# Moving the decay of two chunks from the values to the keys in a fused retention and feed-forward kernel

**Chip, cores, metric.** One core of one Trainium2 chip. The metric is the device time of one execution in microseconds (us), median of several runs; lower is better.

## The reference

Eight heads with a fixed decay each, over four sequences of 768 tokens with 64 values per head; the result goes through a multiplicative feed-forward layer.

```python
gamma = 1.0 - 2.0 ** (-5.0 - np.arange(H))
for t in range(S):
    state = gamma * state + outer(k[:, :, t], v[:, :, t])
    y[:, :, t] = scale * q[:, :, t] @ state
x = y as (tokens, heads * 64)                 # 3072 x 512
out = (((x @ w1) * (x @ w2)) @ w3) @ w_out
```

## The kernel before

The sequence is cut into chunks of 128 tokens. A chunk needs its keys in fp16 (`k16`), the keys transposed and padded (`KP`), scores masked to fp16 (`am`), and padded values (`VP`). The decay inside the chunk is a factor per token and head, `VS` or `VS2`. It is multiplied into the values, once, and so it is in both the output (`am` times `VP`) and the state (`k16` times `VP`). It could just as well be multiplied into the keys: scores and state both contain the keys exactly once. W3 and W_out are folded into one matrix at the start of the kernel.

The change concerns chunks 2 and 3, in the hand-ordered part between the start of the kernel and its steady loop. Each engine runs its instructions in the order of these lines, so this order is the schedule of every engine. A "row group" is one `by_rows` call: the product with a quarter of the rows of W1 or W2. `pa` are copies of W1's sums out of PSUM, where TensorE's results stand ("accumulator copies"). ScalarE, VectorE and GpSimd are `nc.scalar`, `nc.vector` and `nc.gpsimd`; `cast_to(dst, src, True)` is a copy on VectorE, `False` one on ScalarE.

```python
def pair_casts(n, moved, names="kv", eng=None):   # half of a chunk's 128 tokens
    eng = eng or (nc.vector if moved else nc.gpsimd)
    if "k" in names:  ... copy or cast 64x512 of the keys to k16s[n] ...
    for r in range(2 if "v" in names else 0):     # even heads, odd heads
        eng.tensor_tensor(VP[n % 3][to, :, r, ...], values, VS2 broadcast, MULT)
...
by_rows(W1, ps, 0 and 1)                          # feed-forward of chunks 0, 1
for n in (2, 3):
    pair_casts(n, False, "k")                     # GpSimd
    pair_casts(n, True, "k", nc.scalar)
by_rows(W1, ps, 2)                                # "third row group"
transposes(2)
by_rows(W1, ps, 3)
transposes_front(3, "psK")
nc.gpsimd.tensor_copy(W2[0][:, :], w2_st[0][:, :])
pair_casts(2, False, "v")
pair_casts(3, False, "v")
...                                               # pa[0..2] out of PSUM
scores(2, between=lambda: pair_casts(2, True, "v"))
cast_to(pa[3], ps[3], True)
transposes_back(3)
cast_w(W2, w2_st, 1, False)                       # ScalarE; then 2 and 3
...
by_rows(W2, ps, 0); outputs(2, "psK"); scores(3); by_rows(W2, ps, 1); t_new = kv(2, "psY")
pair_casts(3, True, "v")
...                                               # f1.a_unit between W2's row groups
outputs(3, "psA1"); f1.a_unit(6, "psA0"); casts(4); Tst[0] = kv(3, "psK")
f0.o_unit(0)                                      # "first output unit"
```

## Time and profile before

| | before |
|---|---|
| time, median of 3 runs | 194.74 us (194.6 to 195.18) |
| span of the profiled execution | 193.1 us |
| busy: TensorE, VectorE, ScalarE, GpSimd | 184.1, 117.0, 103.3, 83.6 us |
| third row group of W1 ends (the next work starts) | 35.20 us |
| first output unit starts | 46.66 us |
| from there to the end | 146.43 us, TensorE never waiting |

How to read it: TensorE (PE) is busy nearly throughout, so the kernel is as long as TensorE's work plus its holes. A change in chunks 2 and 3 acts between 35.20 and 46.66 us. I call these 11.46 us "the stage".

### The profile page before, as it was taken

The numbers are of one execution on the slowest core, as the hardware profiler recorded it, in microseconds if no ns is written. First come the engines' busy times: TensorE is split into PE (matmuls) and PEld (weight loads), VectorE is DVE, ScalarE is ACT, GpSimd is POOL, SyncE is SP. The second block draws the span as 40 slices with busy tenths as digits, with TensorE's granted clock in tenths as the row PEclk, the third lists the DMA queues.
The fourth block names the chain that finished last, engine by engine and source line by source line (L and its number), as shares of the span: only waits on it lengthen the run. The fifth ranks groups of instructions, "written<-read, shape, count | busy, mean of one in ns | idle before, by whom it ended". The sixth has DMA issues, their size and how long they took to land.

```text
span 193.1 us, 4713 instructions
## 1 busy us (share of the span) xinstructions
PE 184.1 (95%) x1785; PEld 139.8 (72%) x1785; DVE 117.0 (61%) x220; ACT 103.3 (54%) x198; POOL 83.6 (43%) x144
## 2 busy tenths in 40 slices
PE   6698999979999999999999999999999999999993
PEld 2234557778797789777977797788777877887752
DVE  3225479699587758656665676565656665753220
ACT  6478598972454465354635463555355545533322
POOL 7600257728864737476252742863426432200000
PEclk9999999999999999999999999999999999999999
DMA  6999999998999999999999989969979930111104
GB/s 207 349 389 398 326 377 355 368 266 198 235 204 221 199 231 237 144 247 211 231 273 187 223 188 223 206 149 270 199 178 201 206 94 19 59 54 54 38 28 154
DMA packets 84007, 40.54 MB, mean 210 GB/s; under 512 B 61329, under 2 KB 78993, under 8 KB 83985
## 3 DMA queue, kind: packets, MB, share of 16 engines
q1 hardware_dynamic: 83984, 40.25, 88.5%
q8 instruction: 14, 0.23, 0.5%
q14 instruction: 9, 0.07, 0.2%
HBM read 29.36 MB, written 6.29 MB: 185 GB/s over the span
## 4 chain that ended last, share of the span: by engine, by line
PE 81%; DMA 10%; ACT 4%; DVE 2%; SPq 1%; issue 0%
PE psF L537 39%; PE psO L563 21%; DMA q<-in_q_dram 6%; PE psA L466 5%; DMA stg<-in_moe_w_out_dram 5%; PE psY L506 3%; PE psY L507 3%; PE psF L760 2%; PE psY L509 2%; PE psK L489 2%; SPq L62 1%; PE psG L537 1%; PE psO L580 1%; ACT w3o L241 1%; PE psG L760 1%; DVE vp L329 1%
## 5 line engine op out<-in xcount | busy, mean ns | idle before, releaser
L537 PE MATMUL psF<-xt,w 128*128 128x256 f16 (+1 forms) x736 | 85.0, 266 | 0.0
L537 PEld LDWEIGHTS <-w 128*128 128x128 f16 x768 | 68.2, 98 | 7.2
L553 DVE TENSOR_TENSOR ht<-pa,psF 128x256 f16<-128x256 f32 x88 | 36.6, 416 | 22.4 <-PE psF L537 13.1
L547 ACT COPY pa<-psF 128x256 f32<-128x256 f32 x84 | 31.3, 372 | 33.4 <-PE psF L537 33.0
L471 DVE TENSOR_TENSOR am<-psA,keep 128x512 f16<-128x512 f32 x48 | 30.9, 684 | 21.4 <-PE psA L466 21.3
L563 PE MATMUL psO<-w3o,ht 128*128 128x512 f16 x184 | 43.3, 379 | 0.0
L498 POOL TENSOR_TENSOR t<-s,GS 128x512 f16<-128x512 f32 x15 | 19.3, 1285 | 38.7 <-DVE s L497 38.7
L568 ACT ACTIVATE osb<-psO 128x512 f32<-128x512 f32 x23 | 13.7, 598 | 37.3 <-PE psO L563 37.3
L563 PEld LDWEIGHTS <-ht 128*128 128x128 f16 x184 | 17.8, 98 | 16.9 <-DVE ht L806 0.2
L383 POOL TENSOR_TENSOR vp<-v,VS 128x256 f16<-128x256 f32 x40 | 23.8, 617 | 6.9 <-DMA v<-in_v_dram 3.3
L514 DVE TENSOR_TENSOR xt<-psY,YS 128x512 f16<-128x512 f32 x24 | 17.8, 742 | 4.1 <-PE psY L509 3.8
L506 PE MATMUL psY<-am,vp 128*128 128x128 f16 x96 | 16.8, 219 | 0.9 <-POOL vp L329 0.7
L507 PE MATMUL psY<-am,vp 128*128 128x128 f16 x96 | 16.7, 219 | 0.6 <-DVE vp L329 0.6
L466 PEld LDWEIGHTS <-kp 128*128 128x128 f16 x192 | 12.5, 98 | 4.5 <-DVE kp L239 0.2
L338 POOL CAST q<-q 128x1024 f16<-128x1024 f32 x10 | 10.6, 1057 | 11.9 <-DMA q<-in_q_dram 11.9
L379 POOL CAST k<-k 128x512 f16<-128x512 f32 x20 | 12.3, 613 | 5.5 <-DMA v<-in_v_dram 2.4
L497 DVE TENSOR_TENSOR s<-psK,t 128x512 f32<-128x512 f32 x16 | 11.0, 688 | 2.8 <-PE psK L489 2.5
L262 DVE COPY w3t<-psW 128x1024 f16<-128x1024 f16 x8 | 5.5, 690 | 10.9 <-PE psW L270 8.5
L466 PE MATMUL psA<-qTd,kp 128*128 128x128 f16 x144 | 11.1, 219 | 0.0
L509 PE MATMUL psY<-qTd,t 128*128 128x128 f16 x60 | 10.8, 219 | 0.0
L440 ACT COPY kp<-kT 64x512 f16<-64x512 f16 x17 | 10.5, 618 | 0.4
L441 ACT COPY kp<-kT 64x512 f16<-64x512 f16 x17 | 10.5, 615 | 0.4
(87 smaller groups left out, 193.9 us busy)
## 6 DMA issues: line engine op xcount, KB each, us to landing
stg<-in_moe_w_dram SPq DMA_DIRECT2D x16, 512.0 KB, 8.5
q<-in_q_dram SPq DMA_DIRECT2D x12, 512.0 KB, 5.4
out_dram<-osb SPq DMA_DIRECT2D x23, 256.0 KB, 3.2
k<-in_k_dram SPq DMA_DIRECT2D x20, 256.0 KB, 5.3
v<-in_v_dram SPq DMA_DIRECT2D x20, 256.0 KB, 5.5
stg<-in_moe_w_out_dram SPq DMA_DIRECT2D x4, 512.0 KB, 8.2
stg<-in_k_dram SPq DMA_DIRECT2D x2, 512.0 KB, 9.9
stg<-in_v_dram SPq DMA_DIRECT2D x2, 512.0 KB, 9.7
```

The costliest lines, as they stand in the source:

```text
L383: nc.gpsimd.tensor_tensor(vp[:, :, r, r * 64 : r * 64 + 64], v32[:, :].rearrange("j (p s e) -> j p s e", s=2, e=64)[:, :, r, :], VS[:, :]. ...
L466: nc.tensor.matmul(ps[:, i, r, :], lhsT=kp[:, p, r, :], rhs=queries(n, p), start=True, stop=True)
L471: nc.vector.tensor_tensor(am[:, half * 2 : half * 2 + 2, :, :].rearrange("j p s i -> j (p s) i"), ps[:, :, :, :].rearrange("j p s i -> j ( ...
L498: eng.tensor_tensor(t16[:, :, :], s32[:, :, :], GS[:, :, :], MULT)
L506: nc.tensor.matmul(ps[:, p, :], lhsT=vp[:, p, 0, :], rhs=am[:, p, 0, :], start=True, stop=False)
L507: nc.tensor.matmul(ps[:, p, :], lhsT=vp[:, p, 1, :], rhs=am[:, p, 1, :], start=False, stop=(c == 0))
L509: nc.tensor.matmul(ps[:, p, :], lhsT=Tst[0][:, p, :], rhs=queries(n, p), start=False, stop=True)
L514: nc.vector.tensor_tensor(XT[n // 2][:, :, n % 2 * C : (n % 2 + 1) * C].rearrange("p a (i t) -> p a t i", t=2), ps[:, :, :].rearrange(orde ...
L537: nc.tensor.matmul(ps[:, i * w : (i + 1) * w], lhsT=W[d][:, (f + i) * 128 : (f + i + 1) * 128], rhs=XT[self.tok0 // TB][:, d, c0 : c0 + w] ...
L547: nc.scalar.copy(self.pa[f][:, :], ps[:, :])
L553: nc.vector.tensor_tensor(self.HT[:, f : f + TB // self.width, :].rearrange("p f n -> p (f n)"), self.pa.pop(f)[:, :], ps[:, :], MULT,)
L563: nc.tensor.matmul(psO[:, :], lhsT=self.HT[:, f, tb * 128 : (tb + 1) * 128], rhs=W3O[f][:, :], start=(f == 0), stop=(f == 7),)
```

## The change

The intent: at chunk 2's output TensorE waits for values that GpSimd and VectorE are still scaling. So the decay goes onto the keys; values become plain copies, which ScalarE can do too. All four key products are on VectorE, as are both copies of chunk 2's padded keys. ScalarE is relieved of two key casts and of one cast of W2.

```diff
+    def scaled_keys(n, moved):
+        ...
+        nc.vector.tensor_tensor(k16s[n][half], keys, VS2 broadcast, MULT)     # 64x512
+    def plain_values(n, moved, copy):
+        ...
+        copy(VP[n % 3][half, even and odd heads in one pattern], values)      # 64x512
     def transposes_back(n):
-        nc.scalar.copy(kp[0:64, :, 0, :], ps[0:64, :, :])
+        cast_to(kp[0:64, :, 0, :], ps[0:64, :, :], n == 2)
         cast_to(kp[64:128, :, 1, :], ps[64:128, :, :], n == 2)
...
-    for n in (2, 3):
-        pair_casts(n, False, "k")
-        pair_casts(n, True, "k", nc.scalar)
+    scaled_keys(2, False)
+    scaled_keys(2, True)
+    scaled_keys(3, False)
     by_rows(W1, ps, 2)
+    by_rows(W1, ps, 3, blocks=(0, 3))
     transposes(2)
-    by_rows(W1, ps, 3)
-    transposes_front(3, "psK")
+    scaled_keys(3, True)
+    by_rows(W1, ps, 3, blocks=(3, 8))
     nc.gpsimd.tensor_copy(W2[0][:, :], w2_st[0][:, :])
-    pair_casts(2, False, "v")
-    pair_casts(3, False, "v")
+    plain_values(2, False, nc.gpsimd.tensor_copy)
+    plain_values(3, False, nc.gpsimd.tensor_copy)
     cast_to(pa[0], ps[0], False)
-    cast_to(pa[1], ps[1], True)
+    cast_to(pa[1], ps[1], False)
     cast_to(pa[2], ps[2], False)
-    scores(2, between=lambda: pair_casts(2, True, "v"))
+    scores(2)
     cast_to(pa[3], ps[3], True)
-    transposes_back(3)
-    cast_w(W2, w2_st, 1, False)
+    plain_values(2, True, nc.scalar.copy)
+    transposes(3, "psK")
+    nc.gpsimd.tensor_copy(W2[1][:, :], w2_st[1][:, :])
...
-    pair_casts(3, True, "v")
+    plain_values(3, True, nc.gpsimd.tensor_copy)
...                                  # PSUM banks renamed in outputs, scores, a_unit, kv
```

More of the change, by code (lines that the diff above doesn't have):

```diff
@@ L342, in q_cast @@
         q16s[m] = q16
+    def scaled_keys(n, moved):
+        m, c = divmod(n, 2)
+        rows = slice(c * 64, c * 64 + 64)
+        t = 1 - c if moved else c
+        if n not in k16s:
+            k16s[n] = att.tile([128, 512], HP, tag="k16", name="k16", bufs=3)
+        nc.vector.tensor_tensor(
+            k16s[n][t * 64 : t * 64 + 64, :].rearrange("i (h d) -> i h d", d=D),
+            pair_in["k", m][rows, :].rearrange("i (h t d) -> i h t d", t=2, d=D)[:, :, t, :],
+            VS2[rows, t, :].unsqueeze(2).broadcast_to((64, H, D)), MULT,
+        )
+    def plain_values(n, moved, copy):
+        m, c = divmod(n, 2)
+        rows = slice(c * 64, c * 64 + 64)
+        t = 1 - c if moved else c
+        dst = VP[n % 3][t * 64 : t * 64 + 64, :, :, :]
+        dst = bass.AP(dst.tensor, dst.offset, [list(dst.ap[0]), [256, NP], [192, 2], [1, 64]])
+        copy(
+            dst,
+            pair_in["v", m][rows, :].rearrange("j (p s t e) -> j p s t e", s=2, t=2, e=64)[:, :, :, t, :],
+        )
     def q4_cast(half, on_act):
@@ L792 @@
     by_rows(W2, ps, 0)
-    outputs(2, "psK")
-    scores(3)
+    outputs(2, "psA0")
+    scores(3, ("psA1", "psK"))
     by_rows(W2, ps, 1)
@@ L797 @@
     Tst[0] = t_new
-    pair_casts(3, True, "v")
+    plain_values(3, True, nc.gpsimd.tensor_copy)
     f1 = ffn[1]
-    f1.a_unit(0, "psK")
+    f1.a_unit(0, "psA0")
     by_rows(W2, ps, 2)
-    f1.a_unit(2, "psA0")
+    f1.a_unit(2, "psK")
     by_rows(W2, ps, 3)
-    f1.a_unit(4, "psK")
+    f1.a_unit(4, "psA0")
     for i in range(4):
@@ L807 @@
     outputs(3, "psA1")
-    f1.a_unit(6, "psA0")
+    f1.a_unit(6, "psK")
     casts(4)
-    Tst[0] = kv(3, "psK")
+    Tst[0] = kv(3, "psA0")
     f0.o_unit(0)
```

## The prediction

> **What bounds the kernel now.** I read the page first, then the waits of TensorE, then the timelines of single engines around the two chunks that change. The page's row of busy tenths puts TensorE at 9 in nearly every slice after the first fifth, and its chain ends so:
>
> ```profile
> PE 184.1 (95%) x1785; PEld 139.8 (72%) x1785; DVE 117.0 (61%) x220; ACT 103.3 (54%) x198; POOL 83.6 (43%) x144
> PE 81%; DMA 10%; ACT 4%; DVE 2%; SPq 1%; issue 0%
> ```
>
> TensorE is the bound, so a change to the other engines can win only what TensorE now loses to waits. After 46.5 us the view of waits lists none for TensorE. Between 22 and 50 us it lists four, all inside the code that leads to chunk 2's output or just before it:
>
> ```profile
> PE psY L506 <- POOL vp L329: 0.7, 1, 0.7
> PE psY L507 <- DVE vp L329: 0.6, 1, 0.6
> PE psT L450 <- ACT k L324: 0.4, 1, 0.4
> PE psY L506 <- DVE am L471: 0.2, 1, 0.2
> ```
>
> The third belongs to chunk 0, which the change leaves alone. The other three are the target. In TensorE's timeline (start, length, engine, line, operands):
>
> ```profile
> 37.83 0.38 PE L760 MATMUL psG<-xt,w 128*128 128x256 f16 x2
> 38.89 0.22 PE L506 MATMUL psY<-am,vp 128*128 128x128 f16 x1 [0.68 <-POOL vp L329]
> 39.70 0.22 PE L507 MATMUL psY<-am,vp 128*128 128x128 f16 x1 [0.59 <-DVE vp L329]
> ...
> 40.33 0.22 PE L506 MATMUL psY<-am,vp 128*128 128x128 f16 x1 [0.19 <-DVE am L471]
> ...
> 40.66 0.61 PE L466 MATMUL psA<-qT,kp 128*128 128x128 f16 x8
> ```
>
> Chunk 2's output could have begun at 38.05 (37.83 and two matmuls 0.11 apart) and the next work began at 40.66: 2.61 us for twelve matmuls that take 0.70 in chunk 3 (starts 45.29 to 45.99). So 1.91 us are lost there, and 0.21 in chunk 2's scores (start 36.52 to the next work at 37.18, 0.66 against 0.45 for chunk 3's, waiting for the padded keys). The ceiling of the gain is 2.12 us, 1.1% of 194.74: "faster by over 2%" is out of reach even if every wait goes.
>
> Why are the values late? They land at about 37.3, and then two engines scale them at once:
>
> ```profile
> 37.33 2.70 POOL L329 TENSOR_TENSOR vp<-stg,VS 64x256 f16<-64x256 f32 x4 [0.52 <-DMA stg<-in_v_dram]
> 38.07 0.72 DVE L329 TENSOR_TENSOR vp<-stg,VS 64x256 f16<-64x256 f32 x1
> 38.72 0.83 DVE L329 TENSOR_TENSOR vp<-stg,VS 64x256 f16<-64x256 f32 x1
> 43.40 0.42 DVE L329 TENSOR_TENSOR vp<-stg,VS 64x256 f16<-64x256 f32 x1
> 43.51 1.44 POOL L498 TENSOR_TENSOR t<-s,GS 128x512 f16<-128x512 f32 x1 [3.48 <-DVE s L497]
> 43.74 1.49 DVE L329 TENSOR_TENSOR vp<-stg,VS 64x256 f16<-64x256 f32 x1
> ```
>
> The same VectorE instruction takes 0.42 us when it starts first and up to 1.49 beside a GpSimd one; the last of them ends at 45.23, 0.28 after GpSimd's at 44.95.
>
> **What the skill says.** The Trainium skill, "SBUF — State Buffer", section "SBUF: two separate sides": VectorE and GpSimd share one SBUF port pair as an exclusive lock; a VectorE instruction with two SBUF inputs and a GpSimd instruction that reads SBUF block each other for the whole instruction, and the first to start has it. The trace agrees: the blocked end minus the holder's end is 0.28, which is 0.42 less some 0.14 of start-up. It also holds the other way: the first key cast on GpSimd took 0.80 instead of 0.61, because VectorE's product t<-s,GS (33.87 for 0.69) was running. The trace before has no plain GpSimd copy that blocks a VectorE product, so that half rests on the skill. "VectorE: DVE Perf Modes", section "Two Vector instructions with no wait between them", says that an instruction starts only after all earlier ones if an operand begins in another group of 32 partitions than before. In the trace, VectorE's instructions on equal partitions overlap by 0.09 us, and the first one after a change of half starts 0.03 after the end before it (38.07 after 38.04). The new instructions change halves nearly every time, so I add 0.03 and no overlap.
>
> **The change part by part.**
> Removed for chunks 2 and 3: eight half-value products (four on GpSimd at 0.61 uncontended, four on VectorE at 0.42), two key casts on ScalarE (0.62 each) and two on GpSimd (0.61). One 0.58 key copy out of PSUM leaves ScalarE, as does one 1.05 weight cast; ScalarE takes over one 0.58 accumulator copy (0.69 on VectorE).
> Added on GpSimd: three plain 64x512 copies; from its cast of the same form I take 0.61 each, and the 1.04 weight cast. Added on ScalarE: one copy, 0.62. None of these sets the end: values are then ready at about 38.4, well before the masked scores.
> Added on VectorE: four 64x512 products with two SBUF inputs, 0.69 each (from the 128x512 product at 33.87; the free size counts), and a padded-key copy of 0.43. These are the new path: TensorE's transposes, scores and masking all wait for them in series. Before, two engines cast keys in parallel from 34.2 to 35.7.
>
> VectorE in the new order, with no lock met: it is free at about 34.47 (keys landed at 34.2). Product 2a 34.47 to 35.16; 2b 35.19 to 35.88; 3a 35.91 to 36.60; two padded-key copies to 37.52; 3b 37.55 to 38.24. The transposes of chunk 3 then start at 38.28. Nothing on TensorE can pass them. What follows up to the first output unit, from the starts in the timeline: transposes 0.22, four W2 row groups 3.48, two outputs 1.40, chunk 3's scores 0.45, two key-value products 0.44, four a units 1.80; sum 7.79. It begins at 46.07, against 46.66 before: a gain of 0.59, so 194.15.
>
> With the lock: W2's first rows land at about 35.5 (issued at 25.95, and the cast at 35.77 did not wait for them), and now nothing stands before that cast on GpSimd. It arrives during product 2b, waits, and has the lock next: end 35.88 + 1.04 - 0.14 = 36.78. Product 3a ends at 36.78 + 0.55 = 37.33, the key copies at 38.25. Meanwhile the values occupy GpSimd until 38.37, so 3b ends at 38.92 and the transposes start at 38.95. Add 7.79: 46.74, or 0.08 later than before, so 194.8. The masked scores (38.95 to 39.63, second half to 40.22) then stay just ahead of chunk 2's output, which reaches its second half at about 40.4.
>
> The PSUM renaming only follows the new order: the banks it hands over are free before their next use by the times above (psA0 after chunk 2's row scaling at about 41, first used again at 42.3). The waits that appear earlier are inside that later start of chunk 3's transposes: chunk 2's transposes are due at 35.53 (35.20 and three matmuls of W1's last rows) and get their keys at 35.91, 0.4 later; its scores, due at 36.69, get the second key copy at 37.55 without the lock (0.9) and at 38.28 with it (1.6).
>
> **The rivals.**
> First, the exact order of cast and product: if W2 lands after about 35.9, product 3a goes first, and the cast can only delay 3b through the values behind it; I get roughly -0.2. That is decided by a landing time known to a few tenths.
> Second, the designer's hope: values no longer stall the output, and all 2.1 us come back, 192.6. Against it, the serial VectorE work above, 4 x 0.69 + 2 x 0.43, leaves no way for the transposes of chunk 3 to begin before 38.2.
> Third, VectorE or late values become a worse bound. If products on rows of another half cost more than 0.69, or chunk 3's last value copy (behind the 1.27 state product on GpSimd, ready at about 45.4) misses chunk 3's output at about 45.4, a few tenths are added: up to 195.3.
> Fourth, a shift that is swallowed later, by the loads of later chunks. DMA engines are busy near 100% up to about 90 us, but TensorE waits for nothing there, so a shift of half a microsecond should pass through.
>
> **Range and chances.** The lock case (194.8) I hold at about 0.65, the free case (194.15) and what lies between at 0.3, more than that at 0.05. The weighted middle is 194.6. The runs before spread from 194.6 to 195.18, so the 8-in-10 range is 193.9 to 195.2. Two per cent is 3.9 us either way, beyond all of these: within 2% at 0.97.
>
> **What would show it.** In the profile after: the four product rows on VectorE at 0.69 when alone and one of them stretched to 1.4 or so beside GpSimd's W2 cast; TensorE's waits named for the values gone, and in their place waits for VectorE's keys before the transposes and the scores of chunks 2 and 3, summing to about the same 2 us; the first output unit starting between 46.0 and 46.9. Wrong if the products do not lengthen beside GpSimd's plain copies, if the first output unit starts before 45.5, or if TensorE waits after 47 us.

## The result, and the profile after

The changed kernel is slower by a little: 195.28 us median of 4 runs (195.27 to 195.71) against 194.78 (194.6 to 195.18). The ratio is 1.0028, with a 95% interval of 1.0007 to 1.0049. A ratio here is always the mean time of one kernel's fast runs over that of the other's of the same rounds, so it is not quite the ratio of the medians. The forecast of 194.6 was 0.7 too low, and the range ended at 195.2, so it missed.

The page after (engine totals, then the chain by engine) shows next to no change in totals:

```profile
PE 184.2 (95%) x1785; PEld 139.7 (72%) x1785; DVE 117.0 (60%) x220; ACT 101.7 (53%) x196; POOL 82.1 (42%) x142
PE 79%; DMA 11%; ACT 3%; DVE 2%; SPq 2%; issue 1%
```

ScalarE and GpSimd have 1.6 and 1.5 us less to do, and it helps nothing, because neither was the bound. The waits of TensorE after, in the same stretch (22 to 50 us; us in total, times, longest):

```profile
PE psA L491 <- DVE kp L239: 1.2, 2, 0.9
...
PE psT L475 <- DVE k L351: 0.5, 2, 0.3
```

The three waits for the values and masks of chunk 2 are gone; in their place TensorE waits for VectorE alone, for its key products (k) and its padded copies (kp). The line left out is chunk 0's and not part of the change. TensorE's timeline after:

```profile
35.18 0.49 PE L785 MATMUL psF<-xt,w 128*128 128x256 f16 x3
35.90 0.40 PE L475 MATMUL psT<-ident,k 128*128 128x128 f16 x4 [0.23 <-DVE k L351]
...
36.46 0.38 PE L785 MATMUL psG<-xt,w 128*128 128x256 f16 x2
37.79 0.23 PE L491 MATMUL psA<-qT,kp 128*128 128x128 f16 x1 [0.95 <-DVE kp L239]
38.25 0.56 PE L491 MATMUL psA<-qT,kp 128*128 128x128 f16 x7 [0.23 <-DVE kp L239]
39.09 0.40 PE L475 MATMUL psT<-ident,k 128*128 128x128 f16 x4 [0.28 <-DVE k L351]
...
45.05 0.61 PE L562 MATMUL psG<-xt,w 128*128 128x128 f16 x8
45.65 0.23 PE L531 MATMUL psY<-am,vp 128*128 128x128 f16 x1
...
47.00 2.32 PE L588 MATMUL psO<-w3o,ht 128*128 128x512 f16 x10
```

I take the holes from the starts, as the waits in brackets leave out the end of the matmul before. Chunk 2's transposes are due at 35.51 and start at 35.90: 0.39. Its scores are due at 36.68 and done at 38.64 (seven matmuls from 38.25, 0.056 apart), 1.96 for work of 0.45: 1.51. Chunk 3's transposes come at 39.09 instead of 38.64: 0.45. Chunk 3's output is due at 45.50 and starts at 45.65: 0.15. The sum is 2.50 us of holes, where before had 2.12. The stage is 47.00 - 35.18 = 11.82 us against 11.46, 0.36 more; the spans differ by 0.35 (193.43 and 193.08). The time's remaining 0.15 lies inside the spread of the runs.

VectorE and GpSimd after, timelines of the moments that matter:

```profile
35.15 0.69 DVE L351 TENSOR_TENSOR k<-stg,VS 64x512 f16<-64x512 f32 x1
35.55 1.19 POOL L805 CAST w<-stg 128x1024 f16<-128x1024 f32 x1 [3.01 <-DMA stg<-in_moe_w_dram]
35.87 1.41 DVE L351 TENSOR_TENSOR k<-stg,VS 64x512 f16<-64x512 f32 x1
37.31 0.88 DVE L239 COPY kp<-psT 64x512 f16<-64x512 f16 x2
37.21 1.28 POOL L364 CAST vp<-stg 64x512 f16<-64x512 f32 x2 [0.47 <-DMA stg<-in_v_dram]
38.22 0.81 DVE L351 TENSOR_TENSOR k<-stg,VS 64x512 f16<-64x512 f32 x1
44.99 0.61 POOL L364 CAST vp<-stg 64x512 f16<-64x512 f32 x1
```

Chunk 3's first key product (35.87) takes 1.41 us. The same instruction took 0.69 just before it. GpSimd's cast of W2's first rows arrived at 35.55, during the product before; it took 1.19 instead of 1.04, ended at 36.74, and the blocked product ended at 37.28, 0.54 later. The padded copies of chunk 2 and the last product of chunk 3 queue behind it, and that last product meets GpSimd's value copies in its turn (0.81). The copy at 44.99 is chunk 3's last of the values; TensorE's output of chunk 3 starts 0.05 us after it ends.

### The profile page after: what moved, and what is told of

Same layout as the page of the kernel before. It is cut to its first block, busy times and chain, and to the rows that moved or that the text cites. A ratio compares the mean times of both kernels' runs of the same rounds, so it can differ in the third digit from the quotient of the medians.

```text
span 193.4 us, 4703 instructions
## 1 busy us (share of the span) xinstructions
PE 184.2 (95%) x1785; PEld 139.7 (72%) x1785; DVE 117.0 (60%) x220; ACT 101.7 (53%) x196; POOL 82.1 (42%) x142
## 4 chain that ended last, share of the span: by engine, by line
PE 79%; DMA 11%; ACT 3%; DVE 2%; SPq 2%; issue 1%
PE psF L562 39%; PE psO L588 21%; DMA stg<-in_k_dram 6%; PE psA L491 5%; DMA stg<-in_moe_w_out_dram 5%; PE psY L531 3%; PE psY L532 3%; PE psY L534 2%; PE psK L514 2%; SPq L62 2%; DVE k L351 1%; PE psF L785 1%; ACT kp L241 1%; PE psG L562 1%; PE psO L605 1%
```

## The experiments

All gave correct results. The stage (from the end of W1's third row group to the first output unit) comes from each kernel's profile, times and ratios from up to six runs in turn with the kernel before, whose medians were 194.82 (first eight kernels) and 194.86 (last four).

| kernel | group ends | stage | time, median | ratio to before (95%) |
|---|---|---|---|---|
| before | 35.20 | 11.46 | 194.78 | |
| changed | 35.18 | 11.82 | 195.28 | 1.0028 (1.0007 to 1.0049) |
| changed, again | 35.14 | 11.82 | 195.42 | 1.0030 (0.9990 to 1.0071) |
| e1 W2 cast on ScalarE | 35.95 | 10.97 | 195.06 | 1.0002 (0.9988 to 1.0015) |
| e1 again | 35.47 | 11.00 | 194.69 | 0.9990 (0.9958 to 1.0021) |
| e2 W2 cast in quarters | 35.51 | 11.47 | 195.24 | 1.0023 (1.0008 to 1.0038) |
| e3 first copy on ScalarE | 35.11 | 11.25 | 194.81 | 1.0011 (0.9978 to 1.0044) |
| e4 last values early | 35.38 | 11.68 | 195.17 | 1.0013 (0.9998 to 1.0027) |
| e5 chunk 2 only | 35.43 | 10.28 | 193.82 | 0.9949 (0.9937 to 0.9962) |
| e6 chunk 3 only | 35.18 | 11.73 | 195.36 | 1.0026 (1.0011 to 1.0041) |
| e7 combined | 35.16 | 10.84 | 194.45 | 0.9976 (0.9964 to 0.9989) |
| e8 only the order of chunk 3's values | 35.20 | 11.82 | 195.34 | 1.0023 (1.0010 to 1.0036) |
| e9 e5, chunk 3's transposes early | 34.99 | 10.16 | 193.70 | 0.9935 (0.9901 to 0.9970) |
| e10 e9, state product late | 36.90 | 10.10 | 194.14 | 0.9957 (0.9922 to 0.9993) |

**e1: no GpSimd cast beside the product.**

```diff
-    nc.gpsimd.tensor_copy(W2[0][:, :], w2_st[0][:, :])
+    nc.scalar.copy(W2[0][:, :], w2_st[0][:, :])
```

> The changed kernel with the cast of W2's first rows moved from GpSimd to ScalarE, so that nothing on GpSimd reads SBUF while VectorE forms chunk 3's first key product. Theory (the lock of VectorE and GpSimd costs the changed kernel some 0.7 us): that product falls from 1.41 to 0.69 us, chunk 3's transposes start at about 38.4 instead of 39.09, the first output unit at about 46.3 instead of 47.00, time 0.7 us below the changed kernel, 0.4 below before (ratio about 0.998). Rival (the product is slow by itself, because of its rows 64 to 127 or its strides): it stays at 1.4 and the unit at 47.0. Second rival (ScalarE becomes the bound): product 0.69 but the unit still at 46.8 or later, with TensorE waiting for ScalarE.

Measured: the same product, in VectorE's timeline of this kernel, and the cast on ScalarE beside it:

```profile
35.84 1.04 ACT L805 CAST w<-stg 128x1024 f16<-128x1024 f32 x1 [0.77 <-DMA stg<-in_moe_w_dram]
36.63 0.69 DVE L351 TENSOR_TENSOR k<-stg,VS 64x512 f16<-64x512 f32 x1
```

It is back at 0.69 us beside a cast of the same bytes on ScalarE (the two overlap for 0.25 us here, for 0.48 us in the repetition). So neither the rows nor the strides made it slow, but GpSimd's cast. The stage fell by 0.85, to 10.97. The time fell by only 0.22, and the unit started at 46.92 and not at 46.3, because the third row group ended 0.77 later in this profile.

> The kernel with W2's first cast on ScalarE once more, since its first profile had the third row group end 0.77 us later than that of the changed kernel and its time fell by 0.2 only. Theory: stage 10.97 again (10.9 to 11.05), and a time about 0.4 to 0.8 below the changed kernel's of the same call; if its row group ends late again, something in the kernel sets that and not the chance of the loads. Rival: the shorter stage was an effect of the late row group (data already there), and with an early one the stage is 11.4 to 11.8.

The stage was 11.00 with a row group that ended at 35.47, 0.48 earlier than in the first profile; the time, 194.69, was 0.73 below the changed kernel's of the same call. The rival (the short stage comes from the late start) is out: e4 below leaves the cast on GpSimd, its row group ended at 35.38, nearly as late, and its stage is 11.68. The first three key products take 2.10 us in a row without the lock and 2.82 with it; here merged into one line each by VectorE's timeline, first of e1 again, then of the changed kernel again:

```profile
34.75 2.10 DVE L351 TENSOR_TENSOR k<-stg,VS 64x512 f16<-64x512 f32 x3
```

```profile
34.42 2.82 DVE L351 TENSOR_TENSOR k<-stg,VS 64x512 f16<-64x512 f32 x3
```

**The changed kernel again.**

> The changed kernel once more, unaltered, for a second profile. Theory: the stage from the end of W1's third row group to the first output unit repeats (11.82 us within 0.1) while the end of that row group, which hangs on the first loads, may lie anywhere between 35.1 and 36.0 us; the rest after the first output unit repeats at 146.42. So differences of the times of single runs are the loads', differences of the stage are the kernel's. Rival: the stage itself wanders by some tenths, and the comparisons of stages are worth less than they look.

The stage repeats to 0.01. Over all profiles the row group before it ends between 34.99 and 36.90 us. The traces show what that hangs on: in eleven of the fourteen it ends 9.77 to 9.78 us after the first load of keys has landed (at 25.22 to 27.13), in the other three (before, e1's first run, e2) 11.81 to 11.82 us after the second load of queries (at 23.38 to 24.14). These loads are issued before 15 us, well before the edited part. Why they land at different times is not tested, and an influence of the kernel is not excluded: of e1's eleven runs none was under 194.66, while the fastest of the kernel before in the same calls were 194.68 and 194.74, although e1's stage is 0.46 shorter. It is why I compare stages and use the times as a cross-check. That a kernel is faster than before, the times show for e5, e7, e9 and e10 alone.

**e2: the same cast in four pieces.**

```diff
-    nc.gpsimd.tensor_copy(W2[0][:, :], w2_st[0][:, :])
+    for c0 in range(0, 1024, 256):
+        nc.gpsimd.tensor_copy(W2[0][:, c0 : c0 + 256], w2_st[0][:, c0 : c0 + 256])
```

> The changed kernel with the same cast on GpSimd cut into four casts of 256 columns: the same bytes on the same engine, but shorter holds. Theory (a lock held for a whole instruction, taken in turn): VectorE gets its turn after the first quarter, the product takes 0.9 to 1.0 us instead of 1.41, the remaining quarters run between VectorE's copies out of PSUM, the first output unit starts at 46.6 to 46.9. Rival (shared bandwidth, not a lock): the product stays near 1.4. Rival (the product is slow by itself): 1.4 too.

Measured, in narrow windows of the two timelines, the product and the first of the four casts:

```profile
36.19 0.77 DVE L351 TENSOR_TENSOR k<-stg,VS 64x512 f16<-64x512 f32 x1
35.55 0.87 POOL L806 CAST w<-stg 128x256 f16<-128x256 f32 x1 [2.98 <-DMA stg<-in_moe_w_dram]
```

The product took 0.77 us, even less than the 0.9 to 1.0 expected, and ended 0.55 after that cast; the second cast, issued behind it, took 0.86 where the third and fourth took 0.40. The bytes and the engine are the same and only the instruction is shorter, so the block lasts an instruction and is not a shared bandwidth. The stage fell by 0.35 only, to 11.47: chunk 3's last key product now met a copy of the values and took 1.11 us instead of 0.81. The unit started at 46.98, outside the expected interval, since the row group ended 0.33 later.

**e3: one padded copy back on ScalarE.**

```diff
-        cast_to(kp[0:64, :, 0, :], ps[0:64, :, :], n == 2)
+        nc.scalar.copy(kp[0:64, :, 0, :], ps[0:64, :, :])
```

> The changed kernel with one part undone: chunk 2's first padded-key copy is back on ScalarE. Theory (the serial VectorE work is the path to chunk 3's transposes): 0.45 us shorter chain; scores of chunk 2 at about 37.8, transposes of chunk 3 at about 38.4 to 38.6, first output unit 46.4 to 46.6, about 0.5 us below the changed kernel. Rival (the late values, or chunk 3's masks, set the end): unit stays at 47.0 +- 0.1.

The first output unit came at 46.35 (expected 46.4 to 46.6), 0.65 earlier, and the stage was 0.57 shorter at 11.25, although the product still took 1.41. So VectorE's work in series is the path: 0.45 less of it, and a last product that slipped in front of a value copy (0.69 instead of 0.81), come out almost whole.

**e4: chunk 3's last value copy before the state product.**

```diff
     nc.gpsimd.tensor_copy(W2[1][:, :], w2_st[1][:, :])
+    plain_values(3, True, nc.gpsimd.tensor_copy)
...
     Tst[0] = t_new
-    plain_values(3, True, nc.gpsimd.tensor_copy)
```

> The changed kernel with chunk 3's last value copy on GpSimd placed before the state product instead of behind it. Theory (that copy is what holds chunk 3's output for 0.15 us, 45.50 to 45.65): the output follows its predecessor without a gap and the first output unit comes 0.15 us earlier in the stage, no more; in the times barely to be seen. Rival (the state product or the masks hold it): no change.

The stage fell by 0.14, to 11.68. The hole before chunk 3's output was that copy's.

**e5: the change for chunk 2 alone.**

```diff
     scaled_keys(2, True)
-    scaled_keys(3, False)
+    pair_casts(3, False, "k", nc.scalar)
+    pair_casts(3, True, "k", nc.scalar)
...
-    scaled_keys(3, True)
...
-    plain_values(3, False, nc.gpsimd.tensor_copy)
...
     nc.gpsimd.tensor_copy(W2[1][:, :], w2_st[1][:, :])
+    pair_casts(3, False, "v")
+    pair_casts(3, True, "v", nc.gpsimd)
...
-    plain_values(3, True, nc.gpsimd.tensor_copy)
```

> The change for chunk 2 alone: its keys scaled on VectorE and its values copied plainly; chunk 3 back to plain keys (both halves on ScalarE) and scaled values (all on GpSimd, after W2's second cast, needed only at 45). Theory: VectorE has two of the four products, both before the lock can be met; chunk 2's output starts at about 38.8 instead of 40.20, W2's second cast (lands 38.4 to 39.0) then becomes the next wait of a few tenths, first output unit at about 45.6, time about 1.4 us below the changed kernel and 1.0 below before (ratio 0.994 to 0.996). Rival (moving the decay to the keys is itself the loss, since VectorE's work before the scores is then serial): no better than before, unit at 46.6 or later.

As expected to a tenth: unit at 45.71, stage 10.28, time 193.82, ratio 0.9949. What TensorE still waits for in it (waits from 34 to 50 us):

```profile
PE psA L491 <- DVE kp L239: 0.2, 1, 0.2
PE psT L475 <- DVE k L351: 0.2, 1, 0.2
```

W2's second rows, which I had expected to become the next wait, did not: their cast ended at 39.80 and the row group came at 40.18. The idea of moving the decay is therefore good for chunk 2 and bad for chunk 3. In the trace before, the keys of both chunks land at 34.19 and their values at 37.26. TensorE is ready for chunk 2's keys at 35.20, 1.0 us later, and for its values at 38.05, only 0.8 later. It is ready for chunk 3's keys at 36.30, 2.1 us later, but for its values not before 45.29, 8.0 us later. And on VectorE chunk 3's key products stand between chunk 2's and the padded copies.

**e6: the complement.**

```diff
-    scaled_keys(2, False)
-    scaled_keys(2, True)
+    pair_casts(2, False, "k")
+    pair_casts(2, True, "k", nc.scalar)
...
-    plain_values(2, False, nc.gpsimd.tensor_copy)
+    pair_casts(2, False, "v")
...
-    scores(2)
+    scores(2, between=lambda: pair_casts(2, True, "v"))
...
-    plain_values(2, True, nc.scalar.copy)
```

> The complement of the chunk 2 run: chunk 3 with scaled keys and plain values, chunk 2 as before (keys cast on GpSimd and ScalarE, values scaled on GpSimd and VectorE, both padded copies on VectorE). Theory (VectorE's serial work and its meetings with GpSimd set the stage): chunk 2's value products on VectorE again wait for GpSimd's, chunk 2's output is stretched as before, and the stage from the end of W1's third row group to the first output unit is 11.2 to 11.6 us (before 11.46, changed 11.82, chunk 2 alone 10.28). Rival (the loss comes from chunk 2's part of the change): as short as 10.3 to 10.6.

The stage was 11.73, 0.13 above the expected interval and far from the rival's. With the scaled values of chunk 2 back in their meeting with GpSimd (VectorE's second value product took 0.82 us), chunk 3's part of the change loses 0.27 against before. Added to chunk 2's part it loses 1.54 (10.28 to 11.82): the two parts do not add up. In e6 TensorE loses 0.9 us to VectorE's keys and copies before W2's first row group (0.2 before), but then only 1.35 in chunk 2's output (1.91 before), since part of the wait for the values passes meanwhile. In the changed kernel chunk 2's output waits for nothing, so nothing is hidden.

**e8: no decay moved, only the order.**

```diff
-    pair_casts(3, False, "v")
...
-    cast_w(W2, w2_st, 1, False)
+    nc.gpsimd.tensor_copy(W2[1][:, :], w2_st[1][:, :])
+    pair_casts(3, False, "v")
+    pair_casts(3, True, "v", nc.gpsimd)
...
-    pair_casts(3, True, "v")
```

> No decay moved at all: the kernel before with only chunk 3's value products and W2's second cast arranged as in the chunk 2 run (W2's second cast on GpSimd, chunk 3's four value products behind it on GpSimd). Theory (half of the chunk 2 run's gain is GpSimd leaving VectorE alone at 38 to 40 us, half is chunk 2's cheaper values): the second value product on VectorE falls from 0.83 to 0.42, the stage from 11.46 to 10.9 to 11.1, time about 0.5 below before. Rivals: stage 10.3, the order alone is the gain and the moved decay is worth nothing; or stage 11.4, all of the gain is the moved decay of chunk 2.

A miss, and the most instructive one. I had taken chunk 3's value products off GpSimd while VectorE scales chunk 2's values, and put W2's second cast in their place, believing that its rows land at 39.0, as in the trace before (38.99). They landed at 38.51. The timelines of VectorE and GpSimd, and TensorE's wait:

```profile
38.56 1.11 POOL L787 CAST w<-stg 128x1024 f16<-128x1024 f32 x1
38.70 1.25 DVE L329 TENSOR_TENSOR vp<-stg,VS 64x256 f16<-64x256 f32 x1
```

```profile
PE psY L507 <- DVE vp L329: 1.0, 1, 1.0
```

A VectorE product that takes 0.42 alone took 1.25 us: the cast holds longer than the value product it replaced, and the stage was 11.82. So the order of chunk 3's values alone does not give e5's gain; here it loses 0.36. In e5 the same cast does no harm, as chunk 2's values are plain copies on GpSimd and ScalarE and VectorE has no value product to be held. What the order would be worth if the rows landed after VectorE's product is not shown.

**e7: a first try for the best.** It is e5 with `transposes_front(3, "psK")` right after W1's third row group, chunk 2's first padded copy on ScalarE (as in e3), and `cast_to(pa[0], ps[0], True)`.

> A try for the best kernel: chunk 2's part of the change alone, and in addition chunk 3's transposes moved before W1's last row group (their keys need no decay), chunk 2's first padded copy on ScalarE and the first accumulator copy on VectorE. Theory (what is left of the waits is VectorE's key products 0.4 and the two copies in series 0.6): TensorE fills the first with the transposes, the second halves; the stage falls from 10.28 to about 9.9 us, time 0.3 to 0.4 below the chunk 2 run, 1.2 to 1.4 below before. Rival (W2's second rows, landing at 38.7, bound the stage): no better than 10.2.

A miss: stage 10.84, longer than e5's. Chunk 3's transposes now stood first in line and waited for ScalarE's casts of chunk 3's keys (done at 35.54, while the group ended at 35.16), so that all behind them was late. VectorE's accumulator copy (37.70 to 38.39) stood before the masks, and the second half of chunk 2's output came 0.27 late. And the two padded copies did not run side by side. VectorE's timeline:

```profile
37.24 0.43 DVE L239 COPY kp<-psT 64x512 f16<-64x512 f16 x1 [1.43 <-ACT kp L480]
```

VectorE waited for ScalarE's half of the same tile. The halves do not overlap in memory, but the copy waits for a semaphore that ScalarE's instructions set. So the split buys nothing here; in e3 it did, as VectorE was still held by the cast at the time. How much each of the three additions cost was not separated.

**e9: the transposes at the right place.**

```diff
 (e5)
     by_rows(W1, ps, 3, blocks=(3, 8))
+    transposes_front(3, "psK")
...
-    transposes(3, "psK")
+    transposes_back(3)
```

> The chunk 2 run with chunk 3's transposes moved ahead of chunk 2's scores, into TensorE's wait for the padded keys (both copies stay on VectorE). Theory: the 0.22 us of transposes fall into a wait, the stage goes from 10.28 to about 10.06, time 0.2 below the chunk 2 run. Rival (W2's second rows bound the stage, as they land at 38.4 to 39.0): unchanged.

The stage fell by 0.12, to 10.16, where 0.22 was expected. TensorE's timeline:

```profile
36.26 0.38 PE L785 MATMUL psG<-xt,w 128*128 128x256 f16 x2
36.48 0.39 PE L475 MATMUL psT<-ident,k 128*128 128x128 f16 x4
36.70 0.22 PE L491 MATMUL psA<-qT,kp 128*128 128x128 f16 x1
```

No hole is left between W1's last rows and the first score. The other 0.1 came back at once as a new wait: the second half of chunk 2's output was due at 38.74 and started at 38.85, behind VectorE's second mask (done at 38.80). The time, 193.70, is 0.6% below before and beats both kernels; against e5 the difference is too small for the runs to show.

**e10: the state product behind the padded copies.** In addition to e9, VectorE's product of chunk 1's state is issued right after `transposes(2)`.

> As the run with the early transposes, and VectorE's product of chunk 1's state, which stands between the landing of the keys and their scaling, moved behind the padded copies. Theory (VectorE's serial work before the scores is what is left): keys scaled 0.3 earlier, transposes of chunk 2 with next to no wait, stage 9.7 to 9.9. Rival (the product now delays the masks, and chunk 2's output waits for them): 10.1 or more.

The stage was 10.10: the rival's case. The keys came earlier, but the masks, now behind the state product, held chunk 2's output. Its profile had the latest start of all (row group at 36.90), so its time of 194.14 says little about the stage.

## Why the prediction was wrong, point by point

- **The bound and the ceiling: right.** TensorE's holes in one stage are all that could change. In all profiles the part after the first output unit is 146.41 to 146.43 us, so a shift passes through, and the fourth rival is out.
- **VectorE's serial chain: right.** The products took 0.68 and 0.69 us when alone, the copies 0.42 and 0.43, each starting 0.01 to 0.03 after the one before, as added up in the prediction. e3 shows that the chain is the path.
- **The lock case: right in mechanism and nearly in size.** Predicted ends against measured: first product of chunk 3 37.33 and 37.28, padded copies 38.25 and 38.19, last product 38.92 and 39.04, transposes 38.95 and 39.09. That a plain GpSimd cast blocks a VectorE product, which rested on the skill alone, is shown by e1 and e2.
- **What failed first: the weighting of the order of cast and product.** "The lock case (194.8) I hold at about 0.65, the free case (194.15) and what lies between at 0.3": there was no free case. The cast came in the middle of the product before it, 0.3 to 0.4 us from either end, and in all four profiles that leave these two instructions alone (changed, again, e3, e4) the next product took 1.41 us. The working had found this, and the point of 194.6 averaged it away: 0.2 us.
- **What failed second, and more: two mis-sized terms of the lock case,** which ends at 194.8 and would have been too low too. From the row group's end to chunk 3's transposes I had 3.75 us (38.95 - 35.20); it took 3.91 (39.09 - 35.18). Of these 0.16, the two value copies on GpSimd make 0.12: they do not overlap (second start 37.88, 0.06 after the first ends) and so release VectorE later; the wait of TensorE is 0.05 and not 0.03. From the transposes to the first output unit I had 7.79; it took 7.91. That is the third rival's last value copy, ready at 45.60 instead of "about 45.4": a hole of 0.15, confirmed by e4, less 0.03 as the outputs take 0.67 and not 0.70. It was listed as a rival and left out of the sum. Together 0.28: the stage's predicted 0.08 of loss became 0.36. So of the 0.7 us by which 194.6 was too low, 0.2 is the weighting and 0.3 these terms. The other 0.2 is not the stage's: the medians of the kernel before were 194.74 and then 194.78, and 0.15 of the measured difference is not in the spans of the two profiles.
- **The signs that I named: right but for one.** One product stretched to 1.41 ("1.4 or so"), waits for values replaced by waits for keys, no wait after 47 us. The sum of the holes is 2.50 ("about the same 2 us"). The unit, at 47.00, is just outside 46.0 to 46.9.
- **The class and the range.** "Within 2%" was right. The range ended at 195.2, below the 195.3 that I had worked out for the third rival, and 195.28 was measured.

## What to carry to other kernels

Before work moves to another engine, list which of its instructions read two SBUF tensors on VectorE and which GpSimd instructions can be in flight then; a meeting can cost most of the length of the other's instruction (here 0.72 us for a cast of 1.04), and the landing time of a load can decide it. Put a factor on the operand that has more time between its landing and its use, count what else its engine must do in that time, and decide it per chunk: keys for chunk 2 (0.5% faster), values for chunk 3. That rule is read from these two chunks; no run tests it by itself. When the working has found a collision with times, forecast the collision; do not average it with the case without it.

## What the Trainium skill lacked or had wrong

- "SBUF — State Buffer", "SBUF: two separate sides": the exclusive lock is right, and holds for a plain GpSimd cast against a VectorE product (1.41 us instead of 0.69; 0.69 again with the cast on ScalarE). It does not say how long a blocked instruction still needs: the product ended 0.54 us after the cast, where it takes 0.69 alone. Nor does it say who comes next when both have work queued: here they took turns, and a cast cut into four let VectorE in after a quarter (0.77).
- "VectorE: DVE Perf Modes", "Two Vector instructions with no wait between them", gives no cost for an instruction held by a change of partitions: here it started 0.01 to 0.03 us after the end of the one before, instead of some 0.09 before it.
- No page has it: the loads of a kernel's first microseconds landed at different times from profile to profile (the third between 7.4 and 9.1 us), and the start of the same stage moved from 34.99 to 36.90 us with the first keys and queries, while the stage of one kernel repeated to 0.03 us.
